# Attention beside a GELU layer: the order of the first half's bursts, and the bank in which the row maxima are turned

## The chip, the cores and the metric

The kernel runs on one core of one Trainium2 chip. The metric is the device time of one execution in microseconds (us), the median of several executions. The tensor engine (TensorE) is written PE in the profile, its weight loads PEld, the vector engine (VectorE) DVE, the scalar engine (ScalarE) ACT, GpSimd POOL, and the engine that issues the transfers SP.

## The reference

```python
def _A_ref(x, wqkv, wo):            # S = 2048 rows, D = 512, H = 32 heads of Dh = 16
    qkv = (x @ wqkv) ...            # q, k, v: [H, S, Dh]
    scores = jnp.einsum("bhqd,bhkd->bhqk", q, k) * (Dh ** -0.5)
    p = _softmax(scores, axis=-1)
    o = jnp.einsum("bhqk,bhkd->bhqd", p, v)
    return ... o ... @ wo

def _B_ref(x, w1, b1, w2, b2):      # F = 1792
    return gelu(x @ w1 + b1) @ w2 + b2

xn = _layernorm(x)
return x + _A_ref(xn, A_wqkv, A_wo) + _B_ref(xn, B_w1, B_b1, B_w2, B_b2)
```

All inputs and the output are float32. The scores of 32 heads over 2048 by 2048 positions are the bulk of the work.

## The kernel before

**Blocks and units.** The attention is cut into 32 blocks: a group of four heads by a quarter (512) of the queries. A block has 16 units. In the main loop `unit` is called once for each: it does the scores of unit `u` (`s_half`, once for each of the four heads) and, 19 units later (`LEAD`), the transposed scores of the same block's data, unit `e` (`e_half`, four heads).

- A **score** (the page's pS): queries down, keys across, 128 by 512. VectorE takes the row maxima of it (`s_max`, L363). When a block's 16 units are through, `s_end` joins the maxima (mneg, L379), and `store`, half a unit later, turns them with four small matmuls (L386), splits them in two float16 parts (mhl, L389 and L390) and sends them through memory (m_d, L393) into two rows of the query operand (L345).
- A **transposed** score (pT): keys down, queries across, with the maxima already subtracted by those two rows. ScalarE takes its exponential (L410, into pe).
- The **values**' product (pV): float32, of the exponentials with v, for unit `e - 1` or `e - 2`, accumulated over a block's 16 units.
- The **dense** work (pD): the projections, the two layers of B, the output projection, fed in steps from one stream of groups. A group sums into one bank; when it is through, ScalarE reads the bank out (hh, yt, pf, vv).

**Halves of the array.** Each of these products has a depth of 64 (or 62) rows and runs as four 32-column matmuls in the upper or in the lower 64 rows of the array, so that two of different halves run side by side. Heads 0 and 2 are in the upper rows, 1 and 3 in the lower.

**Half units.** A unit has two halves (`a` in `unit`). A half is a **burst** of two scores and two transposed scores, and then the values' product in one half of the array beside three or four dense steps in the other (`dense`; the group's `pace` says how many). In the first half the values are below and the dense steps above, in the second the other way round. The matmuls of values or dense steps wait on a counter, `turns`, which the last of the half unit before has raised.

**The order.** Every engine but the loaders runs the instructions in the order in which the code issues them (a manual schedule). In the first half's burst that is score 0, transposed 1, score 1, transposed 0; in the second score 2, transposed 3, score 3, transposed 2.

**The banks.** PSUM has eight banks. `free_banks` holds lists: three for scores ("S"), three for transposed scores ("T"), one for the dense work, one for the values. `banks(tag)` takes the oldest of a list and puts it back at its end, so that a score waits for the maxima of the score three before it, and a transposed one for the exponential three before. `hold` takes a bank out of a list for as long as a sum lasts: a dense group takes the oldest of "T", and gives its bank back to "T" when it has been read out. A group that ends in the second half of a unit is read out in the first half of the next (`one_more`, ahead of the dense steps), where the next group takes its bank.

Of the kernel before, what the change touches and what calls it, by code (L numbers as in the profile page):

```python
# [19 lines left out]
S = 2048  # L20
# [34 lines left out]
def layer_kernel(ctx: ExitStack, tc: tile.TileContext, x, wqkv, wo, w1, b1, w2, b2, out):  # L55
# [48 lines left out]
    def bank_tile(k, tag):  # L104
        return ps.tile([P, QB], F32, tag=f"B{k}", bufs=1, name="p" + tag)

    def banks(tag):
        k = free_banks[tag].pop(0)
        free_banks[tag].append(k)
        return bank_tile(k, tag)  # L110
# [48 lines left out]
    def given(engine, ns):  # L159
        backlog[engine] += ns  # L160
# [17 lines left out]
    def leave(user, goes_on):  # L178

        p = newest.pop(user, None)  # L180
        if p is not None and goes_on:
            p.then_inc(turns, 1)
            tc.no_tile_sem_insts.add(p.ins.name)
            counted[0] += 1
            left.append(p)

    def enter():

        if left:
            goal[0] = f"turn{counted[0]}"  # L190
            for p in left:
                tc.add_to_no_dep_group(goal[0], p.ins)
            left.clear()

    def tiled(user, dst, lhs, rhs, start, stop):

        for j in range(0, P, 32):
            product(user, dst[j:j + 32], lhs[:, j:j + 32], rhs, start=start, stop=stop)
# [11 lines left out]
    def fetch_scale(m):  # L210

        scale_of[m] = nc.scalar.alloc_register(f"sexp{m}")
        nc.scalar.reg_load(scale_of[m], sexp[0:1, m:m + 1].bitcast(I32))
# [105 lines left out]
    def tick():  # L319
        held[0] = pos[0] < NU and pos[0] % 16 == 0  # L320
        run_due()
        run_steps()
        slot[0] += 1
# [17 lines left out]
    def m_rows(t, h):  # L341
        g, qb = divmod(t, NQB)
        p, a = divmod(h, 2)
        dst = qst[g % 2][qb][64 * a + 62:64 * a + 64, p].rearrange("r (t q) -> r t q", q=P)
        nc.sync.dma_start(dst, m_d[t, 4 * h:4 * h + 4].rearrange("t r q -> r t q"))  # L345
# [20 lines left out]
    def s_half(u, n):  # L366

        s = banks("S")
        s_mm(u, n, s)
        s_max(u, n, s)  # L370

    def s_end(u):

        t, i = divmod(u, 16)
        if i < 15:
            return
        g, qb = divmod(t, NQB)
        mneg = mnegs[t % 2]
        nc.vector.tensor_reduce(mneg[:, :16], mt_of[t].rearrange("p h t k -> p (h t) k"), axis=AX.X, op=ALU.max, negate=True)  # L379
        given("dve", 220)  # L380

        def store():

            pt = banks("S")
            for a in range(2):
                nc.tensor.matmul(pt[32 * a:32 * a + 32, :64], mneg[64 * a:64 * a + 64, :],  # L386
                                 ident[64 * a:64 * a + 64, 64 * a:64 * a + 64], start=True, stop=True)
            mhl = work.tile([64, 2, 64], F16, name="mhl", bufs=2)
            nc.vector.tensor_scalar_mul(mhl[:, 0], pt[:64, :64], 1.0 / MROW)  # L389
            nc.vector.scalar_tensor_tensor(mhl[:, 1], pt[:64, :64], 1.0 / MROW, mhl[:, 0], op0=ALU.mult, op1=ALU.subtract)  # L390
            given("dve", 300)
            for a in range(2):
                nc.sync.dma_start(m_d[t, :, :, 64 * a:64 * a + 64], mhl[32 * a:32 * a + 16])  # L393
            for h in range(4):
                m_rows(t, h)

        stores[t] = store

    def e_half(u, n):

        p, a = divmod(n, 2)
        t, kt = divmod(u, 16)
        g, qb = divmod(t, NQB)
        st = banks("T")
        r = slice(64 * a, 64 * a + 64)
        k0 = (kt % 4) * P
        tiled(None, st, kst[g % 2][kt // 4][r, p, k0:k0 + P], qst[g % 2][qb][r, p, :], True, True)
        pe = work.tile([P, QB], F32, name="pe", bufs=12)
        ptiles[u, n] = pe
        nc.scalar.activation(pe, st, AF.Exp, scale=scale_of[g // 2])  # L410
        given("act", 520)

    def v_half(u, a):

        t, kt = divmod(u, 16)
        g, qb = divmod(t, NQB)
        if kt == 0 and a == 0:
            pv_of[t] = hold("V", "S")
        pv = pv_of[t][0]
        r = slice(64 * a, 64 * a + 64)  # L420
        for h in (2, 3, 0, 1):
            c = (4 * g + h) * VW
            product("V", pv[32 * h:32 * h + 32, :], vv[r, kt, c:c + 32], ptiles[u, h][r],
                    start=(kt == 0 and a == 0), stop=(kt == 15 and a == 1))
# [77 lines left out]
    NU = NG * NQB * 16  # L502
# [155 lines left out]
    def ended(at_once=True):  # L658

        if cur[0] is not None and cur[0].over():  # L660
            done, cur[0] = cur[0], None
            ends.append(done.end)
            if at_once:
                settle()
# [5 lines left out]
    def one_more():  # L670

        if ends:
            ends.pop(0)()
        elif extras:
            extras.pop(0)()
# [10 lines left out]
    def dense(gen, side):  # L686

        f = group(gen)
        for _ in range(0 if f is None else f.pace[pos[0] % 2]):
            if not f.usable(side):  # L690
                return
            f.product(side)
# [25 lines left out]
    def spare(gen, side):  # L718

        if extra[0] is None and not spent[0]:  # L720
            f = next(gen, 0)
            spent[0] = f == 0
            extra[0] = Halves(f) if f else None
        if extra[0] is not None:
            extra[0].product(side)
            if extra[0].at == extra[0].n:
                extra[0] = None
# [17 lines left out]
    def unit(gen):  # L745


        u = pos[0]
        e = u - LEAD
        if e > 0 and e % (2 * NQB * 16) == 0 and e < NU:  # L750
            fetch_scale(e // (2 * NQB * 16))
        pos[0] += 1
        for a in range(2):
            for b in range(2 * a, 2 * a + 2):
                if u < NU:
                    s_half(u, b)
                elif u > NU:
                    spare(gen, b % 2)
                if 0 <= e < NU:
                    e_half(e, b ^ 1)  # L760
            if e >= 0:
                one_more()
                enter()

                w, r = (e - 2, 1) if a == 0 else (e - 1, 0)
                live = 0 <= w < NU
                new = r == 0 and w % 16 == 0
                if live and not new:
                    v_half(w, r)
                dense(gen, 1 - r)  # L770
                if live and new:
                    v_half(w, r)

                for user, goes_on in (("V", live and not (r == 1 and w % 16 == 15)),
                                      ("D", cur[0] is not None and not cur[0].over())):
                    leave(user, goes_on)
                for k in backlog:
                    backlog[k] = max(0, backlog[k] - HALF)
                if live and r == 1:
                    v_end(w)  # L780
                ended(False)

            if a == 0 and u % 16 == 0 and u // 16 - 1 in stores:
                stores.pop(u // 16 - 1)()
        if u < NU:
            s_end(u)
        tick()
# [9 lines left out]
    with ExitStack() as st1:  # L797
# [252 lines left out]
        for w in (1, 0):  # L1050
# [5 lines left out]
            else:  # L1056
                a = add("POOL", 800, lambda wf=wf, i1=i1: nc.gpsimd.tensor_scalar(tl[wf], tl[wf], i1, 0.0, op0=ALU.mult, op1=ALU.add), [h])
                w_ready[w] = add("POOL", 1100, lambda wf=wf, hi=hi, lo=lo: nc.gpsimd.tensor_tensor(lo, tl[wf], hi, op=ALU.subtract), [a], free=[wf])
        a = add("DVE", 90, lambda: nc.vector.tensor_tensor(sexp[:, 0:1], fac0[:, 0:1], fac0[:, 1:2], op=ALU.mult), [chain])
        a = add("DVE", 90, lambda: nc.vector.tensor_scalar_mul(sexp[:, 0:1], sexp[:, 0:1], DH ** -0.5), [a])  # L1060
# [5 lines left out]
        a = add("DVE", 90, lambda: nc.vector.tensor_tensor(amv[:, 2:3], amv[:, 0:1], amv[:, 1:2], op=ALU.max), v_sum)  # L1066
# [3 lines left out]
        for i in range(2):  # L1070
# [6 lines left out]
            else:  # L1077
                b = add("POOL", 1240, lambda key=key: nc.gpsimd.tensor_scalar(
                    tl[key], tl[key], inv_v[:, 0:1], 0.0, op0=ALU.mult, op1=ALU.add), [h])
# [30 lines left out]
        a = add("DVE", 220, maxima, m_last)  # L1110
# [3 lines left out]
        def turn_m():  # L1114
            tl[mkey] = sb_tile(mkey)
            for k in range(2):
# [3 lines left out]
        a = add("PE", 300, turn_m, [a], take=[mkey])  # L1120
        a = add("DVE", 160, lambda: nc.vector.tensor_scalar_mul(mhl[:, 0], tl[mkey][:64, :64], 1.0 / MROW), [a])
        a = add("DVE", 160, lambda: nc.vector.scalar_tensor_tensor(mhl[:, 1], tl[mkey][:64, :64], 1.0 / MROW, mhl[:, 0],
                                                                   op0=ALU.mult, op1=ALU.subtract), [a], free=[mkey])
# [290 lines left out]
    with ExitStack() as st3:  # L1414
# [45 lines left out]
        while pos[0] < NU + LEAD + 2:  # L1460
            more_stacks()
            unit(fil)
# [32 lines left out]
```

## Time and profile before

| | |
|---|---|
| time, median of 3 runs | 1487.3 us (1486.66 to 1488.96) |
| the profiled execution's own time | 1485.57 us |
| its span, first to last instruction | 1483.8 us |
| granted TensorE clock | 0.997 |
| PE, DVE, ACT, POOL busy | 99%, 93%, 85%, 45% of the span |
| row maxima L363, DVE | 2029 + 19, 684 ns each |
| exponentials L410, ACT | 2048, 599 ns each |

Instructions overlap on an engine: two maxima one behind the other take 1.28 us together, not twice 0.684. The ends of matmuls are modelled, so a busy PE may still be held up, and a short wait of PE does not show as idle time; where it was held is read from the distance between the starts. In the timeline a row is a run of equal instructions: start, length, engine, line, operation, count, and in brackets the idle time before it with the instruction that ended it.

### The profile page before, as it was taken

To read this page: it belongs to the slowest core of one execution; us is meant where nothing else is said; L and a number is where in the kernel's file an instruction comes from. 1 tells how busy PE (TensorE), PEld (TensorE's weight loads), DVE (VectorE), ACT (ScalarE), POOL (GpSimd) and SP (SyncE) were. 2 spreads that over 40 slices of the span, in tenths; PEclk is the share of its full clock that TensorE was granted. 3 is DMA by queue.
4 is the path that set the end of the run, shared out by engine and by line. 5 is a ranking of instruction groups with operands and counts; after the bars stand their busy time and mean duration, and the time that the engine had idled before them with its cause. 6 is when DMAs were issued, how large, how long until landed. Compare 5 with 4: busy or idle time off the path is not lost.

```text
span 1483.8 us, 88118 instructions
## 1 busy us (share of the span) xinstructions
PE 1467.1 (99%) x40158; PEld 811.5 (55%) x40158; DVE 1374.5 (93%) x2305; ACT 1259.2 (85%) x2366; POOL 662.2 (45%) x672
## 2 busy tenths in 40 slices
PE   8999999999999999999999999999999999999998
PEld 4445555555555555555555555555555555555554
DVE  7889999999999999999999999999999999999923
ACT  5868888888999888899988889998888998888884
POOL 3202857563787301377831037782115777121100
PEclk9999999999999999999999999999999999999999
DMA  6732556554224210221112111121112110111432
GB/s 213 226 113 70 163 171 195 160 157 144 76 72 114 65 37 23 68 62 41 44 43 87 30 36 44 53 73 44 43 38 80 50 37 21 56 55 31 141 93 95
DMA packets 112623, 124.83 MB, mean 84 GB/s; under 512 B 22908, under 2 KB 84220, under 8 KB 112248
## 3 DMA queue, kind: packets, MB, share of 16 engines
q1 hardware_dynamic: 112248, 119.18, 26.6%
q8 instruction: 314, 5.14, 1.5%
q14 instruction: 61, 0.50, 0.1%
HBM read 81.66 MB, written 37.34 MB: 80 GB/s over the span
## 4 chain that ended last, share of the span: by engine, by line
PE 89%; DVE 8%; ACT 1%; DMA 1%; issue 0%; SPq 0%; DVEq 0%; ACTq 0%
PE pV L169 26%; PE pD L169 25%; PE pS L169 18%; PE pT L169 18%; DVE mt L363 7%; PE pT L992 2%; DMA wq<-in_A_wqkv_dram 1%; PE pD L992 0%; DVE ac L1370 0%; ACT xs L945 0%; PE pT L962 0%; ACT xt L966 0%; DVE xt L975 0%; SPq L858 0%; DVE wvh L1075 0%
## 5 line engine op out<-in xcount | busy, mean ns | idle before, releaser
L363 DVE TENSOR_REDUCE mt<-pS 128x1 f32<-128x512 f32 x2029 | 1296.9, 684 | 44.0 <-PE pS L169 24.3
L410 ACT ACTIVATE pe<-pT 128x512 f32<-128x512 f32 x2048 | 1111.5, 599 | 178.0 <-PE pT L169 84.4
L169 PE MATMUL pV<-pe,vv 64*32 64x512 f32 x8192 | 1072.3, 594 | 0.1
L169 PE MATMUL pT<-qst,kst 64*32 64x512 f16 x8192 | 709.8, 378 | 0.5 <-issue 0.5
L169 PE MATMUL pS<-kst,qst 62*32 62x512 f16 x8116 | 614.3, 378 | 3.6 <-DVE mt L363 2.2
L169 PEld LDWEIGHTS <-qst 62*32 62x32 f16 x8192 | 283.6, 92 | 237.5 <-issue 58.0
L169 PE MATMUL pD<-xb,wc 64*32 64x512 f16 x5376 | 360.9, 377 | 0.0
L169 PEld LDWEIGHTS <-kst 64*32 64x32 f16 x8192 | 269.8, 91 | 159.9 <-issue 69.2
L169 PE MATMUL pD<-w_s,g 64*32 64x512 f16 x5376 | 356.4, 377 | 0.0
L169 PEld LDWEIGHTS pV<-pe,vv 64*32 64x32 f32 x8192 | 182.0, 105 | 88.9 <-PE pV L169 4.5
L169 PE MATMUL pD<-xt,wqk_h 64*32 64x512 f16 x2400 | 157.8, 378 | 0.0
L169 PEld LDWEIGHTS <-wc 64*32 64x32 f16 x5376 | 117.0, 91 | 43.0 <-issue 0.6
L169 PEld LDWEIGHTS <-g 64*32 64x32 f16 x5376 | 113.8, 92 | 41.0
L1337 POOL TENSOR_TENSOR xa<-xa,yt 128x512 f32<-128x512 f32 x16 | 20.4, 1278 | 232.0 <-ACT yt L1335 232.0
L466 POOL TENSOR_TENSOR osb<-osb,rb 128x512 f32<-128x512 f32 x31 | 39.8, 1283 | 165.8 <-DMA rb<-den_d 123.4
L1289 POOL TENSOR_TENSOR t<-hh 128x512 f32<-128x512 f32 x56 | 58.2, 1040 | 86.3 <-ACT hh L1312 85.3
L1291 POOL TENSOR_TENSOR t<-t,hh 128x512 f32<-128x512 f32 x56 | 71.7, 1281 | 4.7
L1284 POOL TENSOR_TENSOR t<-t,hh 128x512 f32<-128x512 f32 x56 | 71.7, 1281 | 4.7
L1283 POOL TENSOR_SCALAR t<-t,gs 128x512 f32<-128x512 f32 x56 | 38.7, 692 | 66.0 <-ACT t L1278 66.0
L1286 POOL TENSOR_TENSOR g<-t,g 128x512 f16<-128x512 f32 x56 | 65.2, 1163 | 4.7
L169 PEld LDWEIGHTS <-wqk_h 64*32 64x32 f16 x2400 | 54.5, 92 | 19.4 <-issue 1.4
L169 PE MATMUL pD<-wo_s,oc 64*32 64x512 f16 x828 | 54.7, 378 | 0.0
(160 smaller groups left out, 874.8 us busy)
## 6 DMA issues: line engine op xcount, KB each, us to landing
wc<-w_d SPq DMA_DIRECT2D x56, 256.0 KB
qk_d<-stg SPq DMA_DIRECT2D x32, 256.0 KB
rb<-den_d SPq DMA_DIRECT2D x124, 64.0 KB
wch<-in_B_w_dram SPq DMA_DIRECT2D x14, 512.0 KB
wch<-in_B_w_dram SPq DMA_DIRECT2D x28, 256.0 KB
w_d<-wsp SPq DMA_DIRECT2D x28, 256.0 KB
kst<-qk_d SPq DMA_DIRECT2D x64, 96.0 KB
qst<-qk_d SPq DMA_DIRECT2D x64, 96.0 KB
```

Of the source, the lines that this page charges most:

```text
L169: p = nc.tensor.matmul(*args, **kw)
L363: nc.vector.reduce_max(mt_of[t][:, n, qt, kb:kb + 1], s, axis=AX.X)
L410: nc.scalar.activation(pe, st, AF.Exp, scale=scale_of[g // 2])
L466: pooled((1280, lambda: nc.gpsimd.tensor_tensor(osb, osb, rb, op=ALU.mult)), (620, lambda: nc.gpsimd.tensor_scalar(ot[:, 0], osb, 1.0, 0.0 ...
L992: nc.tensor.matmul(tl[key], lhs, rhs, start=c + n == 0, stop=(c, n) == (NC - 1, 2))
L1283: pooled((690, lambda: nc.gpsimd.tensor_scalar(t1, t1, 1.0, gs[:, 1:2], op0=ALU.add, op1=ALU.mult)), (1280, lambda: nc.gpsimd.tensor_tenso ...
L1284: (1280, lambda: nc.gpsimd.tensor_tensor(t1, t1, hh, op=ALU.mult)),
L1286: (1160, lambda: nc.gpsimd.tensor_tensor(g[:, 1, f, :], t1, g[:, 0, f, :], op=ALU.subtract)),
L1289: pooled((1040, lambda: nc.gpsimd.tensor_tensor(t1, hh, hh, op=ALU.mult)), (620, lambda: nc.gpsimd.tensor_scalar(t1, t1, 1.0, 1.0 / GELU_A ...
L1291: (1280, lambda: nc.gpsimd.tensor_tensor(t1, t1, hh, op=ALU.mult)),
L1337: add = lambda: nc.gpsimd.tensor_tensor(xa, xa, yt, op=ALU.add)
```

## The change

Two edits. The burst of the first half is issued as transposed 1, score 0, score 1, transposed 0; the second half's stays. And the four small matmuls that turn a block's maxima write a bank of the transposed scores' list in place of one of the scores' list.

```diff
         def store():
-            pt = banks("S")
+            pt = banks("T")
...
         for a in range(2):
-            for b in range(2 * a, 2 * a + 2):
-                if u < NU:
+            for kind, b in ((1, 1), (0, 0), (0, 1), (1, 0)) if a == 0 else ((0, 2), (1, 3), (0, 3), (1, 2)):
+                if kind and 0 <= e < NU:
+                    e_half(e, b)
+                elif not kind and u < NU:
                     s_half(u, b)
-                elif u > NU:
+                elif not kind and u > NU:
                     spare(gen, b % 2)
-                if 0 <= e < NU:
-                    e_half(e, b ^ 1)
```

On PE, the burst of a first half (one unit's, about a third into the program; qst and kst are the operands that hold queries and keys) stood so before, each weight load and its matmul the first of four such pairs:

```order
L169 LDWEIGHTS qst_2_89
L169 MATMUL pS<-kst_2_81,qst_2_89 32x512 [waits DVE_49]
...
L169 LDWEIGHTS kst_2_81
L169 MATMUL pT<-qst_1_88,kst_2_81 32x512 [waits Activation_49]
...
L169 LDWEIGHTS qst_2_89
L169 MATMUL pS<-kst_2_81,qst_2_89 32x512 [waits DVE_49]
...
L169 LDWEIGHTS kst_2_81
L169 MATMUL pT<-qst_1_88,kst_2_81 32x512 [waits Activation_49]
```

and stands so now:

```order
L169 LDWEIGHTS kst_2_81
L169 MATMUL pT<-qst_1_88,kst_2_81 32x512 [waits Activation_49]
...
L169 LDWEIGHTS qst_2_89
L169 MATMUL pS<-kst_2_81,qst_2_89 32x512 [waits DVE_49]
...
L169 LDWEIGHTS qst_2_89
L169 MATMUL pS<-kst_2_81,qst_2_89 32x512 [waits DVE_49]
...
L169 LDWEIGHTS kst_2_81
L169 MATMUL pT<-qst_1_88,kst_2_81 32x512 [waits Activation_49]
```

The first transposed score has moved ahead of the first score; the order of the scores among themselves and of the transposed among themselves is as it was.

On VectorE, around the turn of a block's maxima, nothing moves; only the bank read is another:

```order
 L379 TENSOR_REDUCE mneg_101<-mt 128x16 [waits DVE_49,Pool_49]
 L363 TENSOR_REDUCE mt<-pS 128x1 [waits PE_49] x2
-L389 TENSOR_SCALAR mhl<-pS 64x64 [waits PE_49]
-L390 SCALAR_TENSOR_TENSOR mhl<-pS,mhl 64x64 [waits DVE_49]
+L389 TENSOR_SCALAR mhl<-pT 64x64 [waits PE_49]
+L390 SCALAR_TENSOR_TENSOR mhl<-pT,mhl 64x64 [waits DVE_49]
 L363 TENSOR_REDUCE mt<-pS 128x1 [waits PE_49] x42
```

The two maxima that stand between mneg and mhl are those of the first half of the unit in which the turn is made. The orders on ScalarE, GpSimd and SP are the same as before.

## The prediction

> **What bounds the kernel now.** I read the page first: the span, the busy shares and the chain that ended last.
>
> ```profile
> span 1483.8 us, 88118 instructions
> PE 1467.1 (99%) x40158; PEld 811.5 (55%) x40158; DVE 1374.5 (93%) x2305; ACT 1259.2 (85%) x2366; POOL 662.2 (45%) x672
> PE 89%; DVE 8%; ACT 1%; DMA 1%; issue 0%; SPq 0%; DVEq 0%; ACTq 0%
> ```
>
> PE carries the chain, and VectorE is close behind. The windows (the columns are us, then busy time of PE, PEld, DVE, ACT, POOL) show how close in the steady part, and the line of mneg (L379) how long a block is.
>
> ```profile
> 700.00:900.00 200.00, 199.60 (x5755) 113.12 (x5745) 195.47 (x320) 174.32 (x328) 75.52 (x76) 1.00 0.17 49
> ```
>
> ```profile
> L379 DVE TENSOR_REDUCE mneg<-mt x31: 219/220/222, 131.5 to 1415.1; 128x16 f32<-128x64 f32 x31
> ```
>
> Thirty blocks take 1415.1 - 131.5 = 1283.6 us: 42.79 us a block, 2.674 us a unit, 1.337 us a half. VectorE idles 4.53 us in 200, over 74.8 units 0.06 us a unit. So PE sets the pace, and VectorE would after some 0.06 us more work or delay in each unit.
>
> What a half needs when nothing is late, the timeline shows (V, the values' product, starts each half's long part):
>
> ```profile
> 821.88 0.62 PE L169 MATMUL pV<-pe,vv 64*32 64x512 f32 x4
> ...
> 822.57 0.39 PE L169 MATMUL pT<-qst,kst 64*32 64x512 f16 x4
> ...
> 822.75 0.42 PE L169 MATMUL pS<-kst,qst 62*32 62x512 f16 x8
> ...
> 823.15 0.63 PE L169 MATMUL pV<-pe,vv 64*32 64x512 f32 x4
> ...
> 823.33 1.08 ACT L410 ACTIVATE pe<-pT 128x512 f32<-128x512 f32 x2 [0.28 <-PE pS L169]
> ```
>
> From V to V it is 823.15 - 821.88 = 1.27 us, called 1.28 below. The mean is 1.337, so 0.06 us a half, some 60 us of 512 units, is lost somewhere. The same rows show the place of the first edit. This is a first half after three dense steps: the transposed score (pT), whose half of the array came free first, starts 0.18 us **ahead** of the score that stands before it in program order. Yet ScalarE sits idle 0.28 us and is released by the **score**, 0.76 us after the transposed one started. After four dense steps both start together:
>
> ```profile
> 694.33 0.40 PE L169 MATMUL pT<-qst,kst 64*32 64x512 f16 x4
> 694.35 0.59 PE L169 MATMUL pS<-kst,qst 62*32 62x512 f16 x8
> ...
> 694.85 1.08 ACT L410 ACTIVATE pe<-pT 128x512 f32<-128x512 f32 x2 [0.16 <-PE pS L169]
> ```
>
> There ScalarE starts 0.52 us after it. So the result of the transposed score is told to ScalarE only behind that of the score issued before it: 0.76 - 0.52 = 0.24 us are lost to it after three steps. The Trainium skill, "TensorE: Matmul & The Clock Gate", section "The mechanism", says that matmuls both start and end in program order. For the ends the release by pS agrees; for the starts the 0.18 us disagree, and here the measurement decides.
>
> **Part 1, the burst's order.** It adds and removes nothing, so its price is one of waits. With the transposed score first, its exponential can start 0.24 us earlier after three steps (bounds: 0, and the 0.28 us of idle time), and after four by a share of the 0.16 us of idle time; I take 0.06, since the two start 0.02 apart and only the passing of four results is saved. In an undisturbed half this gains nothing: the exponential is not waited for. It gains where the second half's transposed scores wait for the first half's exponentials, and that is where a dense group changes: the new group has taken the oldest bank of "T", two are left to go round, and the second half waits for the first's. Here is one (ScalarE's hh, L1312, reads the old group's bank):
>
> ```profile
> 887.83 0.62 PE L169 MATMUL pV<-pe,vv 64*32 64x512 f32 x4
> ...
> 888.52 0.39 PE L169 MATMUL pT<-qst,kst 64*32 64x512 f16 x4
> ...
> 888.70 0.42 PE L169 MATMUL pS<-kst,qst 62*32 62x512 f16 x8
> ...
> 889.28 1.08 ACT L410 ACTIVATE pe<-pT 128x512 f32<-128x512 f32 x2 [0.28 <-PE pS L169]
> ...
> 889.93 0.40 PE L169 MATMUL pT<-qst,kst 64*32 64x512 f16 x4
> ...
> 890.25 0.69 ACT L1312 ACTIVATE hh<-pD,b_s 128x512 f32<-128x512 f32 x1
> ...
> 890.42 0.40 PE L169 MATMUL pT<-qst,kst 64*32 64x512 f16 x4
> ...
> 890.63 0.61 PE L169 MATMUL pV<-pe,vv 64*32 64x512 f32 x4
> ...
> 891.93 0.63 PE L169 MATMUL pV<-pe,vv 64*32 64x512 f32 x4
> ```
>
> The two exponentials end at 889.28 + 1.08 = 890.36; the second transposed score of the next burst starts 0.06 later, at 890.42, and V 0.21 after that. The three halves take 891.93 - 887.83 = 4.10 us, where 3 x 1.28 = 3.84 would do: this change of group costs 0.26 us. With the exponentials 0.24 us earlier the wait would all but go; but hh follows right behind on ScalarE, and a half does not go under 1.28. I take 0.14 us, about half of the 0.26 (bounds 0 and 0.26).
>
> How many there are, the read-outs on ScalarE count:
>
> ```profile
> L1312 ACT ACTIVATE hh<-pD,b_s 128x512 f32<-128x512 f32 x56 | 38.8, 693 | 0.0
> ...
> L604 ACT ACTIVATE pf<-pD 128x512 f32<-128x512 f32 x25 | 15.1, 606 | 0.0
> L1335 ACT ACTIVATE yt<-pD 128x512 f32<-128x512 f32 x16 | 9.7, 605 | 0.0
> ...
> L621 ACT ACTIVATE vv<-pD 128x512 f32<-128x512 f32 x5 | 3.0, 606 | 0.0
> ```
>
> Of B's first layer every other group (`f` even) goes by three steps: 28 changes at 0.14. The 16 of its second layer (42 products; paces of three and four, or four with a short end) I put there too: 44 x 0.14 = 6.2 us. The other 28, and the 30 of projections and values, go by four steps: 58 x 0.06 = 3.5 us. Together **-9.7 us** (bounds 0 and 44 x 0.26 + 58 x 0.16 = 20.7).
>
> What is queued behind the moved wait: score 0 and score 1 now stand behind transposed 1, which waits for an exponential and, in a block's first unit, for the maxima's rows (L345, below). The two scores' maxima then start later by what it waits, or by up to 0.06 us where it doesn't. I cost this at nothing, as VectorE idles 0.06 us a unit; if that cover is gone, see the first rival.
>
> **Part 2, the bank of the turn.** The turn at 818.41:
>
> ```profile
> 817.51 0.63 PE L169 MATMUL pV<-pe,vv 64*32 64x512 f32 x4
> ...
> 817.69 1.08 ACT L410 ACTIVATE pe<-pT 128x512 f32<-128x512 f32 x2 [0.28 <-PE pS L169]
> 817.73 1.28 DVE L363 TENSOR_REDUCE mt<-pS 128x1 f32<-128x512 f32 x2
> ...
> 818.41 0.27 PE L386 MATMUL pS<-ident,mneg 64*32 64x64 f32 x3
> ...
> 818.47 0.39 PE L169 MATMUL pS<-kst,qst 62*32 62x512 f16 x3
> ...
> 818.92 0.20 DVE L389 TENSOR_SCALAR mhl<-pS 64x64 f16<-64x64 f32 x1
> ...
> 819.06 0.40 PE L169 MATMUL pS<-kst,qst 62*32 62x512 f16 x4
> ...
> 819.08 0.40 PE L169 MATMUL pT<-qst,kst 64*32 64x512 f16 x4
> ```
>
> ```profile
> 820.60 0.63 PE L169 MATMUL pV<-pe,vv 64*32 64x512 f32 x4
> ...
> 823.08 1.16 SPq L345 DMA_DIRECT2D qst<-m_d  x4
> ```
>
> Because the turn has taken one of the scores' three banks, the second score of its burst waits for the maxima that end at 817.73 + 1.28 = 819.01, and starts at 819.06, 0.59 us after the first. The two halves take 820.60 - 817.51 = 3.09 us instead of 2.56: 0.53 us lost. In a bank of "T" that wait goes. Late next are the exponentials: the last transposed score of the burst now waits for the one that ends at 817.69 + 1.08 = 818.77, 0.31 us before 819.08. VectorE's backlog (mneg, the two mhl) stays, and takes up PE's lead only slowly. I take **-0.30 us** a turn (bounds 0 and 0.53). But where a dense group changes in the same unit, "T" has two banks and the turn takes one of them: a transposed score then waits for the old group's read-out, 0.69 us of ScalarE. I take +0.35 there (bounds 0 and 0.69). With 102 changes in some 480 units, one in 4.7, that is 7 of 31 turns: 24 x -0.30 + 7 x 0.35 = **-4.7 us**. The mhl rows stay where VectorE has them, and the rows' transfer (issued until 824.24) too; the first transposed score that needs them comes some 6.7 us after the turn, at about 825.1, so the 0.3 us by which PE comes earlier should still fit: nothing.
>
> **The sum.** -9.7 - 4.7 = -14.4 us. The profiled execution would go from 1485.57 to 1471.2; the median of the runs stands 1.7 us above it, and 1487.3 - 14.4 = **1472.9 us** is the forecast.
>
> **The rivals.**
> - *VectorE becomes the bound (slower).* Place: the first score of each first half, whose result is now told behind that of the transposed one. It decides when that delay is over VectorE's 0.06 us of idle time a unit. At 0.10 us it costs 0.04 x 512 = 20 us: 1507. For it: 195.47 us busy of 200. Against: after three steps the score starts 0.18 us behind the transposed one anyway, so nothing is added there. By the order of starts of the Trainium skill, "TensorE: Matmul & The Clock Gate", section "The mechanism", a transposed score that waits would hold the score for its whole wait, which is this rival; the rows of 822.57 speak against it. Chance 0.09.
> - *The order brings nothing:* the 0.24 us are something else's, or the halves behind take the lead back. Then only the bank's -4.7: 1482.6. Against: the release named in both ACT rows. Chance 0.12.
> - *The bank brings a loss:* VectorE's backlog eats the -0.30, and the collisions cost 7 x 0.69 = 4.8. With the order's -9.7: 1482.4. Chance 0.12.
> - *Both are off and cancel,* or the waits only move: 1487.3. Chance 0.07.
>
> **How the numbers follow.** The forecast's own chance is 0.60. Its range: at best 44 x 0.20 + 58 x 0.08 = 13.4 for the order and 24 x 0.35 = 8.4 for the bank without collisions, 1465.5; the two middle rivals reach to 1482.6, and 1484 leaves out only what is not faster, and a little of the rest. So 1465 to 1484. Faster by over 0.2% (3 us, about what a measurement of this kernel can tell from no change): 0.60 + 0.12 + 0.12 = 0.84; within it 0.07; slower 0.09.
>
> **What would show it.** Right: in first halves after three steps ScalarE starts about 0.5 us after pT, released by pT; ScalarE's idle time put down to pS (0.28 in a row here) shrinks; at a change of group the second burst's transposed scores lie closer; the second score after a turn starts some 0.2 us, not 0.59, after the first; a block falls from 42.79 to about 42.3 us. Wrong: VectorE's busy share in a steady window up to nearly all of it with blocks no shorter (first rival); or turns at which the transposed score waits for hh or yt more often than 7 times.

## The result, and the profile after

The changed kernel takes **1476.9 us** (median of 5 runs, 1476.24 to 1478.03) against 1487.3 us before (5 runs): 0.9929 of it, 95% interval 0.9919 to 0.9940, or 10.4 us less. The forecast was 1472.9 us, with a range of 1465 to 1484.

The page after: span, busy shares, the chain by engine, and the line of mneg, which marks the blocks.

```profile
span 1475.1 us, 88125 instructions
PE 1458.9 (99%) x40158; PEld 817.6 (55%) x40158; DVE 1356.4 (92%) x2305; ACT 1260.5 (85%) x2366; POOL 662.4 (45%) x672
PE 95%; ACT 2%; DVE 1%; DMA 1%; issue 0%; SPq 0%; DVEq 0%; ACTq 0%
```

```profile
L379 DVE TENSOR_REDUCE mneg<-mt x31: 220/220/222, 131.2 to 1407.5; 128x16 f32<-128x64 f32 x31
```

A block now takes (1407.5 - 131.2) / 30 = 42.54 us, where it took 42.79. VectorE's part of the chain fell from 8% to 1%. In the blocks' part of the program before, 91 of its 98 us lie in the 12 us that end at one of twelve turns; after, 7 us are left, at one turn. So the scores that waited for maxima at a turn are nearly gone from the chain. The steady window:

```profile
700.00:900.00 200.00, 199.94 (x5782) 112.64 (x5772) 193.63 (x322) 175.50 (x330) 77.18 (x78) 1.00 0.17 49
```

VectorE is busy 193.63 us of 200, and was 195.47. It has more idle time, though the blocks are shorter, so it has not become the bound.

**A change of group** after three steps, the same one as in the prediction (hh was at 890.25 before):

```profile
884.21 0.62 PE L169 MATMUL pV<-pe,vv 64*32 64x512 f32 x4
...
884.65 0.61 PE L169 MATMUL pV<-pe,vv 64*32 64x512 f32 x4
...
884.89 0.39 PE L169 MATMUL pT<-qst,kst 64*32 64x512 f16 x4
...
885.08 0.42 PE L169 MATMUL pS<-kst,qst 62*32 62x512 f16 x8
...
885.35 0.63 PE L169 MATMUL pV<-pe,vv 64*32 64x512 f32 x4
...
885.58 1.08 ACT L410 ACTIVATE pe<-pT 128x512 f32<-128x512 f32 x2 [0.20 <-PE pS L169]
...
886.55 0.69 ACT L1312 ACTIVATE hh<-pD,b_s 128x512 f32<-128x512 f32 x1
...
886.71 0.40 PE L169 MATMUL pT<-qst,kst 64*32 64x512 f16 x4
...
886.93 0.61 PE L169 MATMUL pV<-pe,vv 64*32 64x512 f32 x4
...
888.23 0.63 PE L169 MATMUL pV<-pe,vv 64*32 64x512 f32 x4
```

The three halves take 888.23 - 884.21 = 4.02 us instead of 4.10. ScalarE starts 0.69 us after the transposed score, where it was 0.76: 0.07 us came of the expected 0.24. It is still put down to a score. The second transposed score of the next burst still starts right behind the exponentials (885.58 + 1.08 = 886.66, then 886.71).

**A turn** with no change of group, the one that was at 818.41:

```profile
813.67 0.39 PE L169 MATMUL pT<-qst,kst 64*32 64x512 f16 x4
...
814.25 0.63 PE L169 MATMUL pV<-pe,vv 64*32 64x512 f32 x4
...
814.35 1.09 ACT L410 ACTIVATE pe<-pT 128x512 f32<-128x512 f32 x2 [0.20 <-PE pS L169]
...
815.15 0.22 PE L386 MATMUL pT<-ident,mneg 64*32 64x64 f32 x1
...
815.16 0.38 PE L169 MATMUL pS<-kst,qst 62*32 62x512 f16 x2
...
815.36 0.38 PE L169 MATMUL pS<-kst,qst 62*32 62x512 f16 x1
...
815.72 0.60 PE L169 MATMUL pV<-pe,vv 64*32 64x512 f32 x4
...
817.02 0.61 PE L169 MATMUL pV<-pe,vv 64*32 64x512 f32 x1
```

The second score (815.36) starts 0.20 us after the first instead of 0.59, and the two halves take 817.02 - 814.25 = 2.77 us instead of 3.09. The first two rows belong to an ordinary first half after three steps: ScalarE starts 814.35 - 813.67 = 0.68 us after the transposed score.

**A turn where a group changes** (six of the 31):

```profile
940.72 0.63 PE L169 MATMUL pV<-pe,vv 64*32 64x512 f32 x4
...
941.62 0.28 PE L386 MATMUL pT<-ident,mneg 64*32 64x64 f32 x2
...
941.92 0.69 ACT L1312 ACTIVATE hh<-pD,b_s 128x512 f32<-128x512 f32 x1
...
942.66 0.40 PE L169 MATMUL pT<-qst,kst 64*32 64x512 f16 x4
...
942.87 0.61 PE L169 MATMUL pV<-pe,vv 64*32 64x512 f32 x4
```

The last transposed score waits for hh (941.92 + 0.69 = 942.61, then 942.66); the half takes 942.87 - 940.72 = 2.15 us. Before, the same half ran between these two rows, 947.08 - 945.16 = 1.92 us:

```profile
945.16 0.63 PE L169 MATMUL pV<-pe,vv 64*32 64x512 f32 x4
...
947.08 0.60 PE L169 MATMUL pV<-pe,vv 64*32 64x512 f32 x4
```

By the distances between the values' products in the first 30 of the 31 turns, 24 turns without a change of group: the turn's half fell from 1.72 to 1.45 us, the half behind it rose from 1.27 to 1.29. Six with one: from 1.83 to 2.12. Every later count of halves is worked out in the same way, from the starts of the values' products.

**Two things the prediction did not have.** ScalarE's waits after (us, times, longest) and before:

```profile
ACT pe L410 <- PE pS L169: 79.8, 338, 1.0
ACT pe L410 <- PE pT L169: 79.0, 332, 1.2
```

```profile
ACT pe L410 <- PE pT L169: 84.4, 290, 1.6
ACT pe L410 <- PE pS L169: 69.6, 286, 0.6
```

The idle time put down to pS was to shrink, and grew. And PE's waits after name the rows' transfer, which those of before never do (six waits, in five of the blocks):

```profile
PEld L169 <- DMA qst<-m_d: 1.7, 5, 0.8
PE pT L169 <- DMA qst<-m_d: 0.3, 1, 0.3
```

```profile
1331.38 0.40 PE L169 MATMUL pT<-qst,kst 64*32 64x512 f16 x4 [0.26 <-DMA qst<-m_d]
```

### The profile page after: what moved, and what is told of

The parts are those of the page before. It is cut to its first block, busy times and chain, and to the rows that moved or that the text cites. A ratio compares the mean times of both kernels' runs of the same rounds, so it can differ in the third digit from the quotient of the medians.

```text
span 1475.1 us, 88125 instructions
## 1 busy us (share of the span) xinstructions
PE 1458.9 (99%) x40158; PEld 817.6 (55%) x40158; DVE 1356.4 (92%) x2305; ACT 1260.5 (85%) x2366; POOL 662.4 (45%) x672
## 4 chain that ended last, share of the span: by engine, by line
PE 95%; ACT 2%; DVE 1%; DMA 1%; issue 0%; SPq 0%; DVEq 0%; ACTq 0%
PE pV L169 29%; PE pD L169 25%; PE pT L169 19%; PE pS L169 19%; PE pT L992 2%; DMA wq<-in_A_wqkv_dram 1%; PE pD L992 1%; DVE mt L363 1%; ACT pe L410 0%; DVE ac L1370 0%; DMA m_d<-mhl 0%; PE pT L962 0%; ACT xs L945 0%; ACT hh L1312 0%; PE pS L1158 0%
## 5 line engine op out<-in xcount | busy, mean ns | idle before, releaser
L363 DVE TENSOR_REDUCE mt<-pS 128x1 f32<-128x512 f32 x2029 | 1278.9, 684 | 54.9 <-PE pS L169 27.0
L410 ACT ACTIVATE pe<-pT 128x512 f32<-128x512 f32 x2048 | 1111.4, 599 | 168.1 <-PE pS L169 79.8
L169 PEld LDWEIGHTS <-kst 64*32 64x32 f16 x8192 | 276.1, 91 | 154.7 <-issue 62.1
```

What stands on the lines that cost most here:

```text
L169: p = nc.tensor.matmul(*args, **kw)
L363: nc.vector.reduce_max(mt_of[t][:, n, qt, kb:kb + 1], s, axis=AX.X)
```

## The experiments

Each was timed beside the kernel before on its chip (medians 1488.8, 1488.8 and 1489.6 us in the three sets), so ratios are compared, or kernels of one set (e1 to e4, e5 to e8, e9 and e10). The last column is the time of the 27 blocks from the fourth on, in the profiled execution.

| run | us, median | of before, 95% interval | 27 blocks, us |
|---|---|---|---|
| before, after (first trace) | 1487.3, 1476.9 | 0.9929 (0.9919 to 0.9940) | 1152.4, 1142.9 |
| e1 order alone | 1481.5 | 0.9944 (0.9928 to 0.9961) | 1147.4 |
| e2 bank alone | 1486.0 | 0.9982 (0.9973 to 0.9991) | 1150.2 |
| e3 turn's bank chosen | 1476.0 | 0.9907 (0.9891 to 0.9922) | 1142.4 |
| e4 scores first | 1500.8 | 1.0076 (1.0059 to 1.0093) | 1164.1 |
| e5 after again | 1477.2 | 0.9920 (0.9905 to 0.9935) | 1144.1 |
| e6 transposed 0 first | 1483.7 | 0.9965 (0.9951 to 0.9978) | 1146.1 |
| e7 scores last | 1487.0 | 0.9989 (0.9979 to 0.9999) | 1152.2 |
| e8 second half's order and e3 | 1471.3 | 0.9878 (0.9862 to 0.9893) | 1138.1 |
| e9 second half's order | 1471.8 | 0.9884 (0.9863 to 0.9905) | 1137.6 |
| e10 both transposed first | 1471.1 | 0.9873 (0.9851 to 0.9894) | 1139.0 |

### e1 and e2: the two edits apart

e1 has the diff's second edit only, e2 its first (`pt = banks("T")`).

> The first half's order alone; the turn stays in a bank of the scores. The prediction's part 1 (a transposed result is told only behind the score ahead of it, 0.24 us lost after three steps) says -9.7 us against before: about 1477.6. A rival says the 0.24 us were mostly something else, since in the trace of after ScalarE still starts 0.68 us after the transposed score's start in a first half after three steps (814.35 - 813.67) and 0.10 us after the next values' product, against 0.76 and 0.18 before: the result now stands behind the last values' matmuls. Then 0.08 us are saved at each of the 44 changes, 3.5 us: about 1484. If the order brings nothing, 1487.

> The turn's bank alone; the order is that of before. The prediction's part 2 says -4.7 us against before (24 turns at -0.30, 7 at +0.35): about 1482.6. Read from the trace of after, the half of a turn takes 1.46 us where it took about 1.71 (25 turns), and 2.12 where it took 1.83 (6 turns): -6.9 + 1.7 = -5.2, about 1482. A rival: the gain of the bank needs the order, since with the order of before the last transposed score still stands behind two scores; then the turn's half stays near 1.7 us and the time within 2 us of 1487.

e1 stands 0.9944 of before: 8.3 us (5.8 to 10.7), or 7.4 by the medians. That lies between the two sizes expected and nearer to the prediction's 9.7. The half in which a change of group is paid fell at every kind of group (changes away from turns): 1.587 to 1.514 us at hh, 1.58 to 1.49 at yt, 1.50 to 1.45 at pf, 1.53 to 1.48 at vv. With the counts of the prediction: 56 x 0.073 + 16 x 0.09 + 30 x 0.05 = 7.0 us.

e2 gives 2.7 us (1.3 to 4.0), less than the 4.7 forecast and the 5.2 read from the trace of after. Its 24 quiet turns take 1.515 us, where after has 1.454: part of what after gains at a turn is the order's. Turn and next half together go from 2.986 to 2.782 us (24 x -0.204 = -4.9), the six collisions from 3.107 to 3.448 (6 x +0.341 = +2.0): -2.9 us, which is the measured size. The two edits together (8.3 + 2.7 = 11.0) give what after gives (10.4 to 11.9 in its two comparisons). Within these intervals they add up. The traces, one of each, show more: in the last 27 blocks e1 is 5.0 us under before and e2 2.2, together 7.2, and after is 9.5 under it. A quiet turn of after is 0.06 us shorter than one of e2, and these 24 x 0.06 = 1.5 us are gained by the two edits together alone.

### e4: both scores first

```diff
-... in ((1, 1), (0, 0), (0, 1), (1, 0)) if a == 0 ...
+... in ((0, 0), (0, 1), (1, 1), (1, 0)) if a == 0 ...
```

> After, but the first half's burst is score 0, score 1, transposed 1, transposed 0. If a transposed result is told only behind the scores ahead of it, both first-half exponentials start later than in before (0.2 us or more at the first), and every change of group costs more: more than 3.5 us slower than e1's order gains in the other direction, so at least 1480, and up to 1495. If the place of the transposed score in the burst does not matter to when its result is told, about 1477 to 1480, by the bank's gain alone.

1500.8 us, 12 above before and 24 above after, and more than the 1495 that was expected at most. So the place of the transposed score does decide when its result is told. The timeline at a change of group:

```profile
899.53 0.50 PE L169 MATMUL pS<-kst,qst 62*32 62x512 f16 x8
...
899.74 0.50 PE L169 MATMUL pT<-qst,kst 64*32 64x512 f16 x8
...
899.96 0.61 PE L169 MATMUL pV<-pe,vv 64*32 64x512 f32 x4
...
900.26 1.09 ACT L410 ACTIVATE pe<-pT 128x512 f32<-128x512 f32 x2 [0.34 <-PE pT L169]
```

ScalarE starts 0.30 us after the values' product; in after it was 814.35 - 814.25 = 0.10 at the first half before the turn, and in before 823.33 - 823.15 = 0.18. Over the first halves from 300 to 1390 us in which ScalarE had been idle, the medians are 0.104 us with no score ahead (after; e1 the same), 0.163 with one (before), 0.285 with two (e4). One score ahead costs 0.06, two cost 0.18.

### e6: the other transposed score first

```diff
-... in ((1, 1), (0, 0), (0, 1), (1, 0)) if a == 0 ...
+... in ((1, 0), (0, 1), (0, 0), (1, 1)) if a == 0 ...
```

> After, but the first half's burst is transposed 0, score 1, score 0, transposed 1: the transposed score that stands first is now the one in the rows that the values' product has just left, so it starts 0.18 us later after three steps. If a transposed result is told only behind the values' matmuls ahead of it, it loses nothing by that: ScalarE starts about 0.10 us after the next values' product as in after, some 0.5 us after the transposed score, and the time is within 2 us of e5. If it is told from its own end, ScalarE starts 0.2 us or more after the next values' product, every change of group costs about 0.1 us more, and the time is 6 to 10 us above e5.

```profile
883.22 0.61 PE L169 MATMUL pV<-pe,vv 64*32 64x512 f32 x4
...
883.47 0.39 PE L169 MATMUL pS<-kst,qst 62*32 62x512 f16 x4
...
883.65 0.59 PE L169 MATMUL pT<-qst,kst 64*32 64x512 f16 x8
...
884.17 1.09 ACT L410 ACTIVATE pe<-pT 128x512 f32<-128x512 f32 x2 [0.21 <-PE pT L169]
```

The transposed score starts 883.65 - 883.22 = 0.43 us after the last part of the values' product, in the rows which that has left. ScalarE starts 0.95 us after that part and 0.52 after the transposed score. In after (the rows above) the transposed score started 884.89 - 884.65 = 0.24 us after that part, 0.19 us sooner, and ScalarE 885.58 - 884.65 = 0.93 us after it, no more than 0.02 sooner. Over the first halves in which ScalarE had been idle, the medians of its start after the next values' product are 0.091 us here and 0.104 in after. So what holds the first result after three steps is mostly the work ahead of the burst, not a score: 0.16 of the 0.24 us that the prediction put down to the score stay.

The trace also holds the moments at which PE's results were told, the updates of its semaphores, though the views above do not list them. Around the four starts of ScalarE that are shown in the text (us; T a transposed score, S a score):

| run | last of the values' product told | last dense step told | results of the burst told | ScalarE starts |
|---|---|---|---|---|
| before | 822.978 | 823.104 | S0 823.185, T1 823.244, S1 823.304 | 823.333 |
| after | 885.303 | 885.429 | T1 885.488, S0 885.547, S1 885.607 | 885.577 |
| e4 | 899.852 | 899.978 | S0 900.058, S1 900.117, T1 900.176 | 900.265 |
| e6 | 883.878 | 884.004 | T0 884.081, S1 884.140 | 884.169 |

The results are put to the updates in the order of the program, and this fits in all four: ScalarE starts 0.09 us behind the result of the first transposed score. Of the first halves from 300 to 1390 us in which ScalarE had been idle, an update lies as far ahead of its start in 307 of 309 in before, 269 of 271 in after, 324 of 327 in e4 and all 287 in e6; mostly that update is the first behind the dense step's in after and e6, the second in before, the third in e4. In the table's rows, of the burst's results each comes 0.06 us or more behind the one ahead, the first 0.06 to 0.08 behind the dense step's, and that 0.126 behind the values'. So a score ahead costs one such step, 0.06 us, and the rest of the late telling is the values' product and the last dense step. The table also shows why ScalarE's row names a score in before and in after: S1 was told at 823.304 and S0 at 885.547, each 0.03 us before the start, and neither is what ScalarE waited for.

The time, though, is 6.5 us above e5, as the other theory had it. It is not the first exponential, and the changes of group do not cost what that theory says: at those read out by hh the half that pays takes 1.508 us in e6 and 1.509 in e5, and the half behind it, which has the first half's burst, goes from 1.292 to 1.320. The traced execution is the fastest of e6's five (1478.1 us, the others up to 1485.2), and its last 27 blocks are only 2.0 us above e5's; where the rest of the 6.5 us lies no trace here shows. What else changed is which transposed score stands last, and in whose rows; e8 bears on that.

### e7: both scores last

```diff
-... in ((1, 1), (0, 0), (0, 1), (1, 0)) if a == 0 ...
+... in ((1, 1), (1, 0), (0, 0), (0, 1)) if a == 0 ...
```

> After, but the first half's burst is transposed 1, transposed 0, score 0, score 1: both scores' results are told 0.2 to 0.4 us later than in after. If VectorE has no more cover than its 0.06 us of idle time a unit (the prediction's first rival), this costs 0.1 us a unit or more: at least 1490. If the three banks of scores take the delay up, since it is the same in every unit, the time stays within 3 us of e5.

1487.0 us, 9.8 above e5, between the two. In the steady window VectorE's idle time rises:

```profile
700.00:900.00 200.00, 199.89 (x5736) 114.94 (x5726) 189.28 (x319) 174.06 (x326) 75.71 (x77) 1.00 0.18 49
```

Of 200 us it is busy 189.28, so VectorE is not the bound as a whole. With the scores' results later, there are 103 halves in which a score starts within 0.06 us of the end of one of VectorE's maxima and a transposed one within 0.06 us of the end of an exponential; after has 17. But the trace's 8.1 us above e5 in the last 27 blocks are spread thin: 5.3 of them lie in halves away from every change and turn, some 0.01 us each. That the three banks take most of the delay up, and not all, fits; which wait makes the rest is not shown.

### e3 and e5: a turn that avoids the collision

```diff
-            pt = banks("T")
+            pt = banks("S" if given_back[0] == pos[0] else "T")
...
                 free_banks[self.key[1]].append(self.key[0])
+                given_back[0] = pos[0]
```

> After, with the turn in a bank of the scores where a dense group's bank was given back in the same half unit, and in one of the transposed scores' elsewhere. If the 6 collisions cost what the trace of after shows (a turn's half of 2.01 to 2.32 us instead of 1.46), they fall to the 1.73 to 1.92 of before: 6 x 0.3 = 1.8 us less than after, about 1475; up to 3 us less if the bank of the scores costs little there now that the transposed scores come first. The rival, that the collisions' cost is taken back by the halves behind them: 1477, the same as after.

> The changed kernel itself, beside the others on the same chip: 1476.9 us expected, 0.993 of before. In its first trace PE stood still some 0.3 to 0.9 us at 147, 170, 218, 259 and 418 us for nothing that the trace shows, about 3 us together; if that belongs to the new order these places come again, and if not they lie elsewhere or are gone. e3 is read against this run: 1 to 3 us less, or the same.

The six halves fell from 2.12 to 1.86 us, that is 6 x 0.27 = 1.6 us; the medians stand 1.1 us apart, and the intervals overlap (0.9891 to 0.9922, 0.9905 to 0.9935). e3 is of another set than e5. The trace shows the gain; the time of the whole kernel does not settle it.

e5 gives after's time again. PE's pauses, which no semaphore ends, come again at two of their places; the timeline of e5, and then that of e2, which has the order of before:

```profile
149.21 0.39 PE L169 MATMUL pT<-qst,kst 64*32 64x512 f16 x3 [0.79 <-issue]
...
171.97 0.39 PE L169 MATMUL pT<-qst,kst 64*32 64x512 f16 x3 [0.83 <-issue]
```

```profile
147.89 0.39 PE L169 MATMUL pS<-kst,qst 62*32 62x512 f16 x3 [0.46 <-issue]
...
170.91 0.39 PE L169 MATMUL pS<-kst,qst 62*32 62x512 f16 x3 [0.69 <-issue]
```

So they belong to places in the program, not to the new order as e5's expectation would have it: each time three of a burst's first four matmuls come late, a transposed score's in the new order, a score's in the old. Not every execution has them. The first three blocks, where most lie, take 131.2 us in before's trace (which has none there), 133.4 in after's, 133.8 in e2's, 130.2 in e6's (none either).

What the pauses wait for can be read from the traces. The page of e5 has this DMA queue (packets, MB, share of the engines):

```profile
q8 instruction: 314, 5.14, 1.5%
```

Each of its packets has 16,384 bytes, and PE with its weight loads has 2 x 40158 instructions, 313.7 times 256. In the twelve traces PE stands still 34 times from 131 us on for over 0.15 us with "issue" as the reason, and all 34 places are the same one in PE's stream: 193 or 194 instructions behind a multiple of 256, as the trace counts them. Each pause ends 1.15 to 1.62 us after the newest of these packets has come in, where the median over all such places is 2.5. So, by the place and by the time, PE waits there for the next 256 instructions of its own program, whose packet has come late.

The rows' transfer was late at two blocks in e5 and at five in the first trace; in the traces of e1 to e10 it is none (e4) to six (e10), and one in e2, which has the order of before.

### e8, e9 and e10: the second half's order

```diff
-... else ((0, 2), (1, 3), (0, 3), (1, 2)):
+... else ((0, 3), (1, 2), (0, 2), (1, 3)):
```

e9 is after with this edit, e8 has e3's edit too, and e10 is e8 with transposed 2 ahead of score 3.

> e3 with the second half's burst as score 3, transposed 2, score 2, transposed 3: there the upper rows have dense steps before and come free first, so the transposed score in them can start 0.18 us earlier after three steps. If what a change of group still costs (about 0.15 us at 102 places) hangs on how soon the second half's exponentials end, some 0.05 us come back at each: 5 us less than e3, about 1470. If the first half's exponentials alone decide it, the time is e3's, about 1475.

> After, with the second half's burst of e8 (score 3, transposed 2, score 2, transposed 3) and the turn as in after. e8 stood 5.9 us under e5 with two edits, of which the turn's gave 1.1 in e3. If they add up, this is 4.8 us under e5: about 1472.5. If the order only pays where the turn no longer collides, the time is e5's, about 1477.

> e8 with the second half's burst as transposed 2, score 3, score 2, transposed 3, which mirrors the first half's. If a score ahead costs a transposed result 0.06 us here as in the first half, another 1 to 4 us go: 1468 to 1470. But transposed 2 now stands sooner behind the first half's exponentials, and holds score 3 where it waits; if that counts, as e7 lets expect, the time is e8's or above: 1471 to 1475.

All three stand at 1471 to 1472 us, 5 to 6 us under after: the second half's order adds to the change, the turn's choice adds nothing that the times can tell here, and the place of the first transposed score of the second half makes no difference (e10). The reason given ahead of e8 (rows that come free sooner after three steps) is not the cause, for the gain is not there. At the changes read out by hh (26 of each sort, away from turns) the half that pays, with the half ahead and the half behind, takes 4.02 us in e5 after four steps and 3.88 in e9; after three steps it is 4.02 and 4.04, since the half behind rises from 1.31 to 1.38 as the one that pays falls from 1.57 to 1.48. The timeline at a change of group after four steps shows another reason: after, then e8.

```profile
893.60 1.08 ACT L410 ACTIVATE pe<-pT 128x512 f32<-128x512 f32 x2 [0.25 <-PE pT L169]
...
894.74 0.40 PE L169 MATMUL pT<-qst,kst 64*32 64x512 f16 x4
...
894.81 0.39 PE L169 MATMUL pD<-xb,wc 64*32 64x512 f16 x4
894.95 0.61 PE L169 MATMUL pV<-pe,vv 64*32 64x512 f32 x4
```

```profile
889.66 1.09 ACT L410 ACTIVATE pe<-pT 128x512 f32<-128x512 f32 x2 [0.23 <-PE pT L169]
...
890.80 0.40 PE L169 MATMUL pT<-qst,kst 64*32 64x512 f16 x4
...
890.85 0.63 PE L169 MATMUL pV<-pe,vv 64*32 64x512 f32 x4
...
891.02 0.61 PE L169 MATMUL pD<-xb,wc 64*32 64x512 f16 x8
```

In both, the last transposed score waits for the exponentials (893.60 + 1.08 = 894.68; 889.66 + 1.09 = 890.75) and starts 0.05 to 0.06 us later. In after it stands in the upper rows, where the values' product comes next: that starts 0.21 us behind it. In e8 it is transposed 3, in the lower rows of the dense steps, and the values' product starts 0.05 us behind it, the dense steps 0.22. At this change the half falls from 1.44 to 1.26 us. So the wait remains, and is moved to the rows that have slack. e6 did the reverse in the first half (transposed 1, in the values' rows, last) and lost 6.5 us, and in its trace the half that has this burst is longer behind a change; that fits, but no run here separates it from what else e6 moved.

## Why the prediction was right, and where its steps were not

- **Part 1, the count and the place: right.** The gain lies at the changes of group; e1 finds it there, at every kind.
- **Part 1, the 0.24 us: the step that was mis-sized.** "0.76 - 0.52 = 0.24 us are lost to it" counted all of the late telling against the score ahead. e1, e4 and e6 show 0.06 to 0.08 for the score; the rest is the values' product and the last dense step further ahead, which the change leaves where they were. So a change after three steps gave 0.08 us (up to 0.14 in the last blocks' second layer), not 0.14. The 0.06 after four steps was right. Sum 7.0 by the halves and 7.4 to 8.3 by the times, for 9.7.
- **The release:** ScalarE was to start about 0.5 us after pT, released by pT, and its idle time put down to pS to shrink. It starts 0.68 after, and the idle time rose from 69.6 to 79.8 us. The matmul that such a row names is the one whose result came last before the start (S0 at 885.547, 0.03 us before it, in e6's table), and need not be the one that was waited for (T1 at 885.488).
- **Scores behind transposed 1, costed at nothing: held.** VectorE's idle time grew in the steady window. e7 shows that larger delays do cost: the first rival has a price, but not at this delay.
- **Part 2, the second score of a turn: right** (0.20 us, not 0.59). Size: -0.20 us a turn with the next half, by e2, for -0.30; both edits together -0.24.
- **Part 2, the collisions: right**, six instead of seven, +0.34 for +0.35. Sum -2.9 for -4.7.
- **The rows' transfer "should still fit: nothing": wrong in a few blocks.** It was late at five of 31 blocks; the row at 1331.38 shows 0.26 us, the five together at most 1.2 us.
- **The sum.** Part 1 was 1.4 to 2.3 us too large, part 2 about 2.0: -14.4 forecast, -11.0 by e1 and e2 together, -10.4 measured. Neither rival with one part at zero came true. Both parts were too large in the same direction, and the range holds the result without one error making up for another.

## What to carry to other kernels

Where an engine is released through a queue of results told in order, moving a product ahead of one neighbour gains only up to the next slower one ahead: look at everything that stands before it, not at the one the wait names. Where a product must wait for a bank anyway, put it last in the rows whose next work has slack (e9: 5 us for one line of order), and look whether the burst behind then waits instead (after three steps it did, and nothing was gained). And when a wait is moved into a shared list of banks, count the places at which that list is already short.

## What the runs showed of the hardware that was not expected

- Results are told in the order of the program, in steps: 0.06 us or more from one product of a burst to the next, 0.126 from the values' product to the dense step behind it, in the four cases of e6's table. ScalarE's start moves by 0.06 us for one score ahead, by 0.18 for two, and, after three steps, a transposed score that starts 0.18 us sooner is told no sooner (e6: 0.091 us after the next values' product, after: 0.104).
- Starts are not in that order across the halves of the array: in e6 the score that stands second in the program starts at 883.47, the transposed score that stands first at 883.65.
- PE pauses for 0.16 to 1.2 us without a semaphore, 34 times in twelve traces, always 193 or 194 instructions behind a multiple of 256 in its own stream and 1.15 to 1.62 us after the newest packet of queue 8 (314 packets of 16,384 bytes) has come in. It happens in some executions and not in others, whatever the order of the burst, and with it the first three blocks take 130.2 to 134.6 us; the pauses themselves, up to 1.8 us together there, are a part of that spread. Why a packet comes late in some executions stays open.
